# Interleaving MLP stages across batch rows and changing who transposes k and the score operand, in a fused sparse-attention and gMLP kernel

## The chip, the cores and the metric

The kernel runs on one core of one Trainium2 chip. The metric is device time in microseconds (us) of one execution. A profile is of one execution, taken by the hardware profiler; its span (first to last instruction) is 1.7 us shorter than the time of that execution. The granted TensorE clock was 0.96 to 1.00 in the mean over the span in every profile used here. The mean hides something: the clock is 1 except in stretches of 3.4 to 10.2 us in which it is 0.5, and there matmuls of 512 columns start about 427 ns apart in place of 216.

Engine names are those of the profile: PE is TensorE's matmuls and PEld its weight loads, DVE is VectorE, ACT is ScalarE, POOL is GpSimd, SP is SyncE, which only issues DMAs here.

## The reference, cut to what matters

```python
# batch 4, heads 8, sequence 768, head_dim 64; chunks of 32 keys, the 6 best chunks of 24 are kept per query
k_min, k_max = min and max of k over each chunk
ub     = sum over d of max(q * k_min, q * k_max)          # an upper bound of a chunk's score
keep   = the 6 chunks with the largest ub, among the causal ones
scores = q k^T / 8, masked to kept chunks and to causal pairs
x      = softmax(scores) v                                # (4, 768, 512) after joining the heads

h      = relu(x @ w_in)                                   # 512 -> 1024, split into u and v
v_n    = layer norm of v without scale
gated  = u * (w_spatial @ v_n + b_spatial)                # 768 x 768 along the sequence
out    = gated @ w_out                                    # 512 -> 512, float32
```

The kernel handles the 32 heads as 16 pairs. Four pairs make one batch row of attention, and each row then goes through the MLP. So the MLP of row b runs beside the attention of row b+1, and the MLP of the last row runs alone at the end.

## The kernel before: the parts that the change and the argument touch

Work is written as small functions that are hung on "beats", 12 to a pair; a scheduler orders each engine's instructions from them. The parts of one pair that matter are these (cuts are marked with `# ...`):

```python
NB = 4
kh_ring = [[ring.tile([P, S], F16, name=f"kh{i}_{hi}") for hi in range(2)] for i in range(NB)]
later = cp.tile([P, 2, 2 * NCH - CPT], F16)
# ...
def init_kh(i):                       # constant half of the key operand
    for hi, (d0, d1) in enumerate(HALF):
        nc.sync.dma_start(out=kh_ring[i][hi][d0:d1, :], in_=expand)

def k_transpose(self):                # pairs 0 to 5 on PE, the rest by DMA transpose from SP
    if self.i < 6:
        self.kT = kT = ps_ml.tile([P, S], F16, tag="mlp", name="kTp")
        for t in range(NQT):
            nc.tensor.transpose(kT[:, t * P:(t + 1) * P], self.k[:, t], identity)
    else:
        self.kT = sb.tile([P, S], F16, tag="kT", name="kT", bufs=3)
        nc.sync.dma_start_transpose(out=self.kT..., in_=self.k...)

def k_max(self):                      # k_min likewise; both on DVE
    nc.vector.tensor_reduce(self.kmm[:, 0, :], self.kT..., axis=AX.X, op=Alu.max)

def a_transpose(self, hi):            # score operand (query and chunk selection): PE, then ACT copies it to SBUF
    self.tr = self.trans_tile()
    for t in range(NQT):
        nc.tensor.transpose(self.tr[:, t * P:(t + 1) * P], self.qs[:, t, 2 * hi:2 * hi + 2, :], identity)

def triangle(self, hi):               # causal mask on the diagonal blocks; row 0 does it on PE instead
    if self.b == 0:
        return
    # ...
    nc.gpsimd.affine_select(out=blk, in_=blk, ...)

def x_transpose(self):
    # ...
    if 4 <= self.i < NPAIR - 1:
        nc.sync.dma_start_transpose(out=dst..., in_=self.x16...)     # xT, read by the MLP's v and u groups
    else:
        # six PE transposes and a DVE copy
```

All loads of q, k, v and of the weights convert float32 to float16 and are issued from POOL, which also runs the triangles. All DMA transposes (k, xT, and the gated product's gT) and the output stores are issued from SP, in one queue.

The MLP of a row is a list of steps: per 128 rows a v group (4 matmuls, ACT relu, DVE statistics), a u group (4 matmuls, ACT relu), an s group (6 matmuls, DVE gate, DMA transpose gT) and an o group (4 matmuls, ACT copy, store). They are spread evenly over the 48 beats of the next row's attention:

```python
for ti in range(NQT): v_group(ti)
for ti in range(NQT):
    u_group(ti)
    if ti >= 1: norm_group(ti - 1)
norm_group(NQT - 1)
for ti in range(NQT): s_group(ti)
for ti in range(NQT): o_group(ti)          # with a lag of 4 beats
# ...
first, count = (b + 1) * HP * BEATS + 9, HP * BEATS
```

Buffers: three PSUM buffers (`ps_ml`) that the MLP groups rotate through.

The softmax here doesn't subtract the row's maximum and nothing guards it: scores larger than these inputs give would overflow.

## Time and profile before

| | before |
|---|---|
| median time | 223.69 us at first, 224.07 us with a fourth run (223.66 to 225.91) |
| span of the profile | 221.8 us |
| PE, DVE, ACT, POOL busy | 88%, 69%, 74%, 36% |

The first lines are from the page of the kernel before: span, busy time by engine, two rows in 40 equal slices of 5.5 us (the granted clock and the busy share of the DMA engines, in tenths, where 9 is 90% or more), and the chain of waits that ended last, by engine.

```profile
span 221.8 us, 5296 instructions
PE 194.7 (88%) x2022; PEld 118.6 (53%) x2022; DVE 153.0 (69%) x453; ACT 163.8 (74%) x335; POOL 80.3 (36%) x99
...
PEclk9999999997999999999999999999999999999998
DMA  6999999999999999967992059428210334520375
...
PE 44%; DMA 18%; DVE 17%; ACT 9%; POOL 7%; issue 3%; POOLq 0%; ACTq 0%; DVEq 0%; SPq 0%
```

The DMA engines are full for about 100 us, then have room.

Busy time of PE overstates its work, because matmuls overlap: one of 512 columns is shown 379 ns long in the mean, but the next starts 216 ns after it. "PE work" below is the number of matmuls times the spacing at which they start when nothing holds them: 216 ns for 512 columns, 162 for 384, 108 for 256, 102 for 240, 56 for 128, and 25 and 29 to 30 for the 48 and 65 columns of the small ones. These are read from the instruction timeline. All 2022 matmuls of the kernel before make about 180 us.

The next view is the table of stretches of the kernel before: start and end, length, and the busy time and count of each engine. The cuts are the first exponential of pair 0, 4, 8 and 12 and the last exponential of all.

```profile
0.00:16.50 16.50, 5.64 (x52) 4.50 (x53) 8.58 (x29) 4.73 (x7) 15.28 (x24) 1.00 1.50 130
16.50:49.90 33.40, 29.54 (x443) 22.75 (x442) 27.09 (x88) 29.39 (x63) 23.75 (x33) 1.00 2.19 162
49.90:99.40 49.50, 44.26 (x489) 27.43 (x489) 45.43 (x133) 38.32 (x84) 21.10 (x22) 0.97 1.99 146
99.40:145.60 46.20, 44.47 (x470) 26.36 (x469) 34.46 (x110) 40.19 (x86) 12.38 (x12) 1.00 0.83 104
145.60:187.40 41.80, 41.69 (x419) 24.43 (x418) 23.38 (x69) 36.82 (x75) 6.95 (x8) 1.00 0.35 77
187.40:221.80 34.40, 29.11 (x156) 13.14 (x154) 14.10 (x28) 14.39 (x27) 0.86 (x1) 0.98 0.42 119
```

The five pairs of columns after the length are PE, PEld, DVE, ACT and POOL; then follow the granted clock, the DMA share and GB/s. I call these stretches the start, the no-MLP stretch, the third, fourth and fifth stretch, and the tail. In the third stretch DVE is busy 45.4 of 49.5 us.

Views of waits, here and below, are cut to the lines that the text uses; `...` marks lines left out between or before them. The last view is who waited for whom between 46 and 64 us in the kernel before, when pair 4 is at work: total us, times, longest.

```profile
POOL w_out_sb L355 <- DMA vt_80<-in_v_dram: 4.2, 1, 4.2
ACT e L263 <- PE sc L258: 3.8, 2, 2.2
PEld L281 <- POOL e L270: 2.7, 1, 2.7
PE acc L281 <- POOL e L270: 2.2, 1, 2.2
DVE kmm L177 <- DMA kT<-k: 2.2, 1, 2.2
```

There are two trails in it. DVE stood for the transposed k of pair 6, which took 9.9 us from issue to landing. POOL stood 4.2 us in the issue of a weight load, and PE later stood 2.2 us for POOL's triangle.

### The profile page before, as it was taken

The numbers are of one execution on the slowest core, as the hardware profiler recorded it, in microseconds if no ns is written. First come the engines' busy times: TensorE is split into PE (matmuls) and PEld (weight loads), VectorE is DVE, ScalarE is ACT, GpSimd is POOL, SyncE is SP. The second block draws the span as 40 slices with busy tenths as digits, with TensorE's granted clock in tenths as the row PEclk, the third lists the DMA queues.
The fourth block names the chain that finished last, engine by engine and source line by source line (L and its number), as shares of the span: only waits on it lengthen the run. The fifth ranks groups of instructions, "written<-read, shape, count | busy, mean of one in ns | idle before, by whom it ended". The sixth has DMA issues, their size and how long they took to land.

```text
span 221.8 us, 5296 instructions
## 1 busy us (share of the span) xinstructions
PE 194.7 (88%) x2022; PEld 118.6 (53%) x2022; DVE 153.0 (69%) x453; ACT 163.8 (74%) x335; POOL 80.3 (36%) x99
## 2 busy tenths in 40 slices
PE   0377999887699989999799999999999999999990
PEld 0266776664366655556455565666555655444430
DVE  6455998968689999998469967773478354376510
ACT  2416999996598888589799997799999876576033
POOL 7992688692695263107111241111111122000000
PEclk9999999997999999999999999999999999999998
DMA  6999999999999999967992059428210334520375
GB/s 39 184 166 150 134 174 150 185 178 147 167 153 161 145 137 138 162 96 126 202 213 57 3 42 114 82 52 210 109 40 1 38 71 92 206 95 0 75 130 224
DMA packets 111273, 26.89 MB, mean 121 GB/s; under 512 B 105872, under 2 KB 107664, under 8 KB 111248
## 3 DMA queue, kind: packets, MB, share of 16 engines
q0 software_dynamic: 76512, 12.19, 84.7%
q1 hardware_dynamic: 34736, 14.36, 33.4%
q8 instruction: 16, 0.26, 0.5%
q14 instruction: 9, 0.07, 0.1%
HBM read 24.38 MB, written 6.29 MB: 138 GB/s over the span
## 4 chain that ended last, share of the span: by engine, by line
PE 44%; DMA 18%; DVE 17%; ACT 9%; POOL 7%; issue 3%; POOLq 0%; ACTq 0%; DVEq 0%; SPq 0%
PE mlp L380 27%; PE sc L258 7%; DMA k<-in_k_dram 7%; PE acc L281 5%; DMA kT<-k 4%; ACT e L263 4%; DMA gT<-g 3%; DVE kmm L177 3%; DMA xT<-x_1868 3%; DVE kmm L181 2%; ACT o L429 2%; PE tr L244 2%; POOL qs_83 L330 2%; DVE vn L404 1%; POOL k L321 1%
## 5 line engine op out<-in xcount | busy, mean ns | idle before, releaser
L263 ACT ACTIVATE e<-sc 128x512 f16<-128x512 f32 x192 | 98.0, 557 | 19.2 <-PE sc L258 16.2
L380 PE MATMUL mlp<-w_in_sb,xT 128*128 128x512 f16 x192 | 51.8, 379 | 1.2 <-DMA xT<-x_1868 1.2
L270 POOL TENSOR_SCALAR_AFFINE_SELECT e<-e 128x768 f16<-128x768 f16 x24 | 21.5, 896 | 81.5 <-ACT e L263 81.4
L281 PEld LDWEIGHTS <-e 128*128 128x128 f16 x672 | 31.2, 98 | 19.5 <-POOL e L270 2.7
L380 PE MATMUL mlp<-vn,wsT 128*128 128x512 f16 x144 | 39.1, 379 | 0.0
L419 DVE SCALAR_TENSOR_TENSOR g<-mlp,b_col,u 128x512 f16<-128x512 f32 x24 | 17.9, 748 | 12.8 <-PE mlp L380 11.5
L380 PE MATMUL mlp<-w_out_sb,gT 128*128 128x512 f16 x96 | 26.0, 379 | 0.0
L380 PEld LDWEIGHTS <-xT 128*128 128x128 f16 x192 | 17.0, 98 | 15.2 <-DMA xT<-x_1868 1.7
L429 ACT COPY o<-mlp 128x512 f32<-128x512 f32 x24 | 14.1, 590 | 14.2 <-PE mlp L380 10.5
L392 DVE BATCH_NORM_STATS2 stats<-vraw 128x6 f32<-128x512 f32 x24 | 16.6, 691 | 8.2 <-ACT vraw L390 8.1
L390 ACT ACTIVATE vraw<-mlp 128x512 f32<-128x512 f32 x24 | 14.4, 600 | 5.3 <-PE mlp L380 5.3
L380 PEld LDWEIGHTS <-wsT 128*128 128x128 f16 x144 | 12.9, 97 | 10.1
L319 POOL DMA_DIRECT2D k<-in_k_dram x14 | 14.5, 1051 | 4.2 <-DMA kT<-k 1.7
L412 ACT ACTIVATE u<-mlp 128x512 f16<-128x512 f32 x24 | 14.8, 619 | 1.4 <-PE mlp L380 1.4
L281 PE MATMUL acc<-vt_80,e 128*128 128x65 f16 x252 | 14.1, 195 | 1.2 <-DVE x_1662 L289 0.8
L281 PE MATMUL acc<-vt_81,e 128*128 128x65 f16 x252 | 12.9, 194 | 1.2 <-DVE x_984 L289 1.2
L404 DVE TENSOR_SCALAR vn<-vraw,mv,rstd 128x512 f16<-128x512 f32 x24 | 13.1, 602 | 0.6 <-ACT rstd L402 0.6
L380 PEld LDWEIGHTS <-gT 128*128 128x128 f16 x96 | 8.6, 97 | 7.5 <-DMA gT<-g 0.8
L288 DVE RECIPROCAL rec<-acc 128x6 f32<-128x6 f32 x32 | 5.9, 186 | 8.8 <-PE acc L281 8.6
L261 PE MATMUL sc<-tri,identity 128*128 128x128 f16 x48 | 11.1, 232 | 0.0
L220 PEld LDWEIGHTS <-rq 128*128 128x128 f16 x160 | 8.4, 99 | 5.1 <-issue 2.1
L177 DVE TENSOR_REDUCE kmm<-kT 128x24 f16<-128x768 f16 x10 | 9.4, 941 | 2.2 <-DMA kT<-k 2.2
(225 smaller groups left out, 379.2 us busy)
## 6 DMA issues: line engine op xcount, KB each, us to landing
out_dram<-o SPq DMA_DIRECT2D x24, 256.0 KB, 2.3
k<-in_k_dram POOLq DMA_DIRECT2D x14, 192.0 KB, 11.1
vt_80<-in_v_dram POOLq DMA_DIRECT2D x3, 384.0 KB, 9.3
qs_84<-in_q_dram POOLq DMA_DIRECT2D x6, 192.0 KB, 8.9
vt_81<-in_v_dram POOLq DMA_DIRECT2D x3, 384.0 KB, 10.0
ws_raw<-in_moe_w_spatial_dram POOLq DMA_DIRECT2D x6, 192.0 KB, 7.7
w_in_sb<-in_moe_w_in_dram POOLq DMA_DIRECT2D x8, 128.0 KB, 5.4
qs_85<-in_q_dram POOLq DMA_DIRECT2D x4, 192.0 KB, 8.6
```

Of the source, the lines that this page charges most:

```text
L177: nc.vector.tensor_reduce(self.kmm[:, 0, :], self.kT.rearrange("d (c ch) -> d c ch", ch=CHUNK), axis=AX.X, op=Alu.max)
L258: mm(sc[:, col:col + n], lhsT=self.kh[hi][:, t * P:(t + 1) * P], rhs=self.a[hi][:, q0:q0 + n], start=True, stop=not diag)
L263: nc.scalar.activation(out=self.e[hi][:, g * 512:g * 512 + width], in_=sc[:, 0:width], func=Act.Exp, scale=scale)
L270: nc.gpsimd.affine_select(out=blk, in_=blk, compare_op=Alu.is_ge, fill=0.0, base=0, channel_multiplier=-1, pattern=[[0, NQT], [1, P]])
L281: mm(self.av[:, qi, :], lhsT=self.e[hi][:, c:c + P], rhs=self.v[hi][:, t, 0:D + 1], start=first and n == 0, stop=last and n == len(blocks) ...
L319: nc.gpsimd.dma_start(out=t[:, :, :, 1 - hi, :].rearrange("p x t d -> p (x t) d"), in_=source(k, b, h, 2))
L380: mm(st[group][:, 0:cols], lhsT=lhsT, rhs=rhs, start=(j == 0), stop=(j == n - 1))
L392: nc.vector.bn_stats(stats, st["vraw"][:, ti, :])
L404: nc.vector.tensor_scalar(st["vn"][:, ti, :], in0=st["vraw"][:, ti, :], scalar1=st["mv"][:, ti, 0:1], scalar2=st["rstd"][:, ti, :], op0=Al ...
L412: nc.scalar.activation(st["u"][:, ti, :], h, func=Act.Relu)
L419: nc.vector.scalar_tensor_tensor(g, in0=vs, scalar=b_col[:, ti:ti + 1], in1=st["u"][:, ti, :], op0=Alu.add, op1=Alu.mult)
L429: nc.scalar.copy(o_sb, o_ps)
```

## The change

Its intent: make the score operand by DMA in the second half, where the DMA engines have room, and take k off the DMA engines, which are full in the first half; put the output matmuls of a row between the v groups of the next row; and do three small things (one mask matmul per pair for five, a cheaper start of the key operand, later weight loads). Cut to its core:

```diff
     def init_kh(i):
+            if i < 2:
+                nc.scalar.copy(kh_ring[i][hi][d0:d1, :], expand)
+            else:
+                nc.sync.dma_start(out=kh_ring[i][hi][d0:d1, :], in_=expand)
-            nc.sync.dma_start(out=kh_ring[i][hi][d0:d1, :], in_=expand)

         def k_transpose(self):
-            if self.i < 6:
+            if self.i < 16:

         def bounds(self):
+            mm(ub[:, 0:(NQT - 1) * W], lhsT=sub_chunk, rhs=later, start=True, stop=False)
             for qi in range(1, NQT):
                 # ... two matmuls per qi
-                mm(ub[:, (qi - 1) * W:qi * W], lhsT=sub_chunk, rhs=later[:, :, ...], start=False, stop=True)

         def a_transpose(self, hi):
+            if hi == 0:
+                self.a = sb.tile([P, NQT, 2, P], F16, tag="a", name="a")
+            if self.i >= 8:
+                if hi == 0:
+                    nc.sync.dma_start_transpose(out=self.a..., in_=self.qs...)
+                return
         # ... a_copy returns at once for those pairs

-        for ti in range(NQT): v_group(ti)      # ... u, norm, s, o of one row after the other
+        return v_, u_, n_, s_, o_
+    pending = [[] for _ in range(NQT)]
     for b in range(B):
+        v_, u_, n_, s_, o_ = mlp(b)
+        steps = sum(pending[:2], [])           # two o groups of the row before
+        for ti in range(NQT):
+            steps += v_[ti]
+            if ti + 2 < NQT:
+                steps += pending[ti + 2]       # the other four between the v groups
+        # ... u with norm, then s; o only for the last row
+        pending = o_
-        first, count = (b + 1) * HP * BEATS + 9, HP * BEATS
+        first, count = (b + 1) * HP * BEATS + 13, HP * BEATS

-        at(12 + 8 * j, load_w_in, j)           # and w_spatial 36 -> 44, w_out 62 -> 76,
+        at(20 + 8 * j, load_w_in, j)           # spatial transposes 60 + 2 so -> 66 + 3 so
```

## The prediction

> **What bounds it now.** The page has TensorE (PE) busy 88%, but busy overstates it, so I price its 2022 matmuls by the start-to-start spacing in the timeline: 216 ns for 512 columns, 56 for 128, 30 for 65, 25 for 48. The Trainium skill ("TensorE: Matmul & The Clock Gate", Back-to-back issue gap) gives N/2.4 + 2.5 ns; the trace agrees at 512 and 128. Sum: 180 us of the 222 us span; granted clock 0.99. The rest is 16 us of start, about 5 us of output at the end, and stalls. By stretches between the first exponentials of pairs 0, 4, 8, 12 and the last exponential (timeline, windows):
>
> - 0–16.5: start.
> - 16.5–49.9 (no MLP): ScalarE busy 29.5, PE work 24.
> - 49.9–99.4: VectorE busy 45.9, ScalarE 38, PE work 41. VectorE bounds it; idle time includes 2.2 us for a k transpose by DMA that took 9.9 us (in the chain).
> - 99.4–145.6: PE work 42.9, ScalarE 40.3; 3.3 us lost, partly on an xT transpose by DMA of 6.1 us (in the chain).
> - 145.6–187.4: PE work 41.0.
> - 187.4–221.8: MLP alone, about 29 us PE work at 216 ns a matmul, then evictions and stores.
>
> **What the change does.**
>
> - PE: 96 query transposes go, 60 k transposes come, 80 small mask matmuls become 16 of 240 columns (102 ns each, estimate from the spacing): −5.4 + 3.4 − 0.4 = −2.4 us net.
> - ScalarE: 16 copies of about 0.8 us go; four 64x768 copies come in the start, where it waits anyway.
> - VectorE: 20 key operand copies read PSUM (about 0.54 us) instead of SBUF (often 0.36, up to 0.9): up to +3.
> - DMA: ten k transposes and four operand loads leave the saturated first half (DMA row full to about 105 us); eight double-sized query transposes come, each with about ten beats (10 us) to land. Weight loads go later, so q, k, v come sooner and the triangle on POOL waits less behind DMA issues.
> - Interleaving moves MLP work, it does not remove it. By the instruction order of both kernels, PE work in the four stretches goes 24→24, 40→36, 43→40, 41→39, and in the tail 29→36. VectorE's work in the third stretch falls from about 47 to 40 us (same durations), because fewer gates and fewer k reductions lie there. Output matmuls no longer follow right behind their gT transposes, and v groups get four more beats for xT.
>
> **Sum.** Start 16.5→16.3; no-MLP 33.4→33; VectorE-bound 49.5→43; next 46.2→42; next 41.8→39.7; tail 34.4→41. Span 215, time about **216.5 us** (−3.2%), range **211.5 to 220.5**. Faster by over 2%: 0.75; within 2%: 0.21; slower: 0.04. The tail gives back more than half of what the attention stretches gain.
>
> **Right or wrong would show as:** last exponential near 174 us (now 187.4); tail about 6.5 us longer with PE spacing still 216 ns; no wait for a k transpose by DMA, and the xT wait after 100 us gone; ScalarE busy down about 10 us; PE stalls in the third stretch still several us, since VectorE and not PE bounds it.
>
> **What could make it wrong.** Query transposes by DMA landing later than ten beats, above all pairs 8 and 9 while loads still fill the DMA engines, or queued behind other SP issues: scores would wait. Every k tile now holds one of the three PSUM buffers that MLP groups rotate through, so matmuls could wait for evictions. VectorE reading k from PSUM could lengthen the third stretch. If DMA supply binds the first 100 us, lighter DMA gains more than I count. Tail stalls at the v/o interleave would add to the end.

## More of the kernel before

Most runs of one kernel lie within about 1% of each other here, and the ratios compare runs of the state "fast" alone. Two runs of the kernel before were "slow" (227.24 and 226.51 us); they count only in the medians of the column "before, same rounds".

The chain, followed back from the last instruction, spends only 44% of the span on PE, though PE is "88% busy". It spends 18% on DMAs and 17% on DVE.

Pair 5 began 13.4 us after pair 4, with 7.4 us of PE work in between.

## The result, and the profile after

The changed kernel took 211.72 us (median of 4 runs, 210.93 to 212.05) against 224.07 us. A ratio is the mean time of one kernel's fast runs over that of the other's in the same rounds, so it is not quite the ratio of the medians: 0.943, with a 95% interval of 0.937 to 0.949. That is a gain of 5.7%, where 3.2% was forecast.

From the page of the changed kernel, the same lines as before:

```profile
span 209.2 us, 5074 instructions
PE 187.0 (89%) x1922; PEld 114.8 (55%) x1922; DVE 154.1 (74%) x453; ACT 155.7 (74%) x323; POOL 79.6 (38%) x99
...
PEclk9999999999999999999999999999999999999998
DMA  6999999999999699979998932948792115530365
...
PE 65%; ACT 17%; DVE 5%; POOL 5%; DMA 4%; issue 3%; POOLq 0%; ACTq 0%
```

DVE does as much as before and PE only slightly less (about 177 us of work against 180). What changed is the chain: DMA went from 18% to 4% of the span, DVE from 17% to 5%, and PE from 44% to 65%. The stretches of the changed kernel, cut at the same events and with the same columns:

```profile
0.00:16.70 16.70, 5.66 (x49) 4.50 (x50) 8.60 (x29) 8.04 (x12) 15.49 (x24) 1.00 1.48 111
16.70:49.20 32.50, 27.93 (x430) 21.41 (x428) 28.81 (x98) 29.51 (x63) 23.34 (x32) 1.00 2.27 164
49.20:89.00 39.80, 38.35 (x468) 25.60 (x468) 36.18 (x115) 35.44 (x77) 21.48 (x24) 1.00 1.94 138
89.00:130.00 41.00, 40.53 (x429) 24.37 (x426) 36.46 (x109) 34.72 (x76) 11.77 (x13) 1.00 1.10 142
130.00:169.20 39.20, 38.97 (x378) 22.45 (x375) 26.11 (x74) 33.40 (x72) 6.63 (x8) 1.00 0.60 112
169.20:209.20 40.00, 35.60 (x188) 16.48 (x186) 17.89 (x33) 14.57 (x26) 0.86 (x1) 0.98 0.42 119
```

Against the prediction's sum:

| stretch | before | predicted | after | after minus predicted |
|---|---|---|---|---|
| start | 16.5 | 16.3 | 16.7 | +0.4 |
| no MLP | 33.4 | 33 | 32.5 | −0.5 |
| third | 49.5 | 43 | 39.8 | −3.2 |
| fourth | 46.2 | 42 | 41.0 | −1.0 |
| fifth | 41.8 | 39.7 | 39.2 | −0.5 |
| tail | 34.4 | 41 | 40.0 | −1.0 |
| span | 221.8 | 215 | 209.2 | −5.8 |

More than half of the miss lies in the third stretch. Of its four pairs, pair 4 alone went from 13.4 us to 6.8. The waits between 46 and 64 us in the changed kernel show why:

```profile
POOL w_out_sb L366 <- DMA vt_80<-in_v_dram: 1.8, 1, 1.8
...
PE sc L269 <- ACT e L274: 0.9, 3, 0.4
...
ACT e L274 <- PE sc L269: 0.7, 3, 0.3
```

Neither a wait of DVE for k nor one of PE for a triangle is left.

### The profile page after: what moved, and what is told of

It reads as the page before. It is cut to its first block, busy times and chain, and to the rows that moved or that the text cites. A ratio compares the mean times of both kernels' runs of the same rounds, so it can differ in the third digit from the quotient of the medians.

```text
span 209.2 us, 5074 instructions
## 1 busy us (share of the span) xinstructions
PE 187.0 (89%) x1922; PEld 114.8 (55%) x1922; DVE 154.1 (74%) x453; ACT 155.7 (74%) x323; POOL 79.6 (38%) x99
## 4 chain that ended last, share of the span: by engine, by line
PE 65%; ACT 17%; DVE 5%; POOL 5%; DMA 4%; issue 3%; POOLq 0%; ACTq 0%
PE mlp L391 38%; PE sc L269 11%; ACT e L274 9%; PE acc L292 8%; ACT a L260 3%; DMA k<-in_k_dram 3%; PE ub L225 2%; POOL qs_83 L341 2%; PE kTp L173 2%; PE tr L208 1%; DVE vn L415 1%; POOL k L332 1%; ACT o L440 1%; DMA out_dram<-o 1%; ACT u L423 1%
## 5 line engine op out<-in xcount | busy, mean ns | idle before, releaser
L391 PE MATMUL mlp<-w_in_sb,xT 128*128 128x512 f16 x192 | 52.9, 379 | 0.0
L281 POOL TENSOR_SCALAR_AFFINE_SELECT e<-e 128x768 f16<-128x768 f16 x24 | 20.8, 867 | 68.7 <-ACT e L274 68.6
L391 PE MATMUL mlp<-vn,wsT 128*128 128x512 f16 x144 | 37.3, 379 | 0.0
L391 PE MATMUL mlp<-w_out_sb,gT 128*128 128x512 f16 x96 | 25.1, 379 | 0.0
L391 PEld LDWEIGHTS <-wsT 128*128 128x128 f16 x144 | 12.9, 98 | 10.4
L181 DVE TENSOR_REDUCE kmm<-kTp 128x24 f16<-128x768 f16 x16 | 15.1, 945 | 3.4 <-PE kTp L173 3.2
L423 ACT ACTIVATE u<-mlp 128x512 f16<-128x512 f32 x24 | 14.3, 597 | 1.7 <-PE mlp L391 1.5
L185 DVE TENSOR_REDUCE kmm<-kTp 128x24 f16<-128x768 f16 x16 | 15.1, 943 | 0.0
L173 PE MATMUL kTp<-identity,k 128*128 128x128 f16 x96 | 8.6, 230 | 6.3 <-POOL tri L144 5.9
L391 PEld LDWEIGHTS <-gT 128*128 128x128 f16 x96 | 9.1, 98 | 8.9
L415 DVE TENSOR_SCALAR vn<-vraw,mv,rstd 128x512 f16<-128x512 f32 x24 | 11.8, 544 | 2.2 <-ACT rstd L413 2.1
```

What stands on the lines that cost most here:

```text
L181: nc.vector.tensor_reduce(self.kmm[:, 0, :], self.kT.rearrange("d (c ch) -> d c ch", ch=CHUNK), axis=AX.X, op=Alu.max)
L185: nc.vector.tensor_reduce(self.kmm[:, 1, :], self.kT.rearrange("d (c ch) -> d c ch", ch=CHUNK), axis=AX.X, op=Alu.min, negate=True)
L281: nc.gpsimd.affine_select(out=blk, in_=blk, compare_op=Alu.is_ge, fill=0.0, base=0, channel_multiplier=-1, pattern=[[0, NQT], [1, P]])
L391: mm(st[group][:, 0:cols], lhsT=lhsT, rhs=rhs, start=(j == 0), stop=(j == n - 1))
L423: nc.scalar.activation(st["u"][:, ti, :], h, func=Act.Relu)
```

## The experiments

Two lists of kernels were made: the kernel before with one part of the change alone (b_), and the changed kernel with one part undone (u_) or with something new (n_). The table holds the result of every run. "Pair 4" is the time from the first exponential of pair 4 to that of pair 5, with the PE work in it in brackets; "pair 8" likewise. The tail is what follows the last exponential. Kernels of one block ran together on one chip, with the kernel before in the same rounds; compare across blocks by the ratio.

| run | median us | before, same rounds | ratio (95%) | pair 4 | pair 8 | third stretch | tail |
|---|---|---|---|---|---|---|---|
| before | 224.07 | | 1 | 13.4 (7.4) | 13.3 (11.4) | 49.5 | 34.4 |
| changed | 211.72 | 224.07 | 0.943 (0.937–0.949) | 6.8 (4.9) | 9.6 (9.7) | 39.8 | 40.0 |
| b_k | 223.17 | 224.84 | 0.995 (0.988–1.003) | 9.4 (7.6) | 16.0 (11.3) | 45.5 | 33.6 |
| b_a | 223.81 | 224.84 | 0.998 (0.992–1.004) | 14.3 (6.7) | 20.2 (10.7) | 50.6 | 33.5 |
| b_mlp | 221.49 | 224.84 | 0.988 (0.983–0.994) | 10.9 (5.0) | 9.8 (9.4) | 45.7 | 41.3 |
| b_w | 225.09 | 224.84 | 1.003 (0.995–1.011) | 16.2 (6.7) | 12.7 (11.4) | 52.2 | 34.3 |
| u_mlp | 216.23 | 224.03 | 0.965 (0.958–0.972) | 9.3 (7.7) | 16.2 (10.8) | 45.4 | 33.4 |
| u_a | 219.18 | 224.03 | 0.978 (0.973–0.984) | 6.8 (4.9) | 10.5 (10.4) | 40.7 | 41.0 |
| u_k | 222.05 | 224.03 | 0.990 (0.982–0.997) | 14.5 (4.9) | 8.7 (8.5) | 49.2 | 40.4 |
| u_small | 213.33 | 224.03 | 0.952 (0.945–0.959) | 7.7 (5.8) | 9.6 (9.7) | 40.0 | 40.3 |
| u_mlp_x | 214.05 | 224.89 | 0.952 (0.949–0.956) | 9.3 (7.7) | 13.0 (11.2) | 45.5 | 33.4 |
| u_k_tri | 226.55 | 224.89 | 1.008 (1.005–1.012) | 9.9 (6.5) | 8.8 (8.5) | 51.3 | 41.0 |
| n_k12 | 218.85 | 224.89 | 0.972 (0.968–0.976) | 6.8 (4.9) | 10.0 (9.7) | 46.0 | 41.5 |
| n_a4 | 223.24 | 224.89 | 0.994 (0.989–0.998) | 7.6 (4.9) | 9.9 (9.8) | 45.3 | 40.7 |
| n_k12b | 212.77 | 225.98 | 0.942 (0.936–0.947) | 6.8 (4.9) | 10.0 (9.7) | 39.9 | 41.3 |
| n_kb | 211.73 | 225.98 | 0.938 (0.932–0.944) | 6.8 (4.9) | 9.6 (9.7) | 39.9 | 40.1 |
| u_mlp_o | 216.54 | 225.98 | 0.957 (0.949–0.965) | 9.3 (7.7) | 16.5 (10.8) | 45.7 | 32.5 |
| u_mlp_xo | 211.64 | 225.98 | 0.937 (0.932–0.942) | 9.3 (7.7) | 11.7 (11.2) | 46.0 | 32.6 |
| n_ob | 210.09 | 224.63 | 0.936 (0.932–0.940) | 6.8 (4.9) | 9.6 (9.7) | 39.9 | 39.2 |
| n_after | 211.40 | 224.63 | 0.942 (0.938–0.945) | 6.8 (4.9) | 9.6 (9.7) | 39.9 | 40.0 |

Some matmul records can be missing from a trace, so the work in brackets can be a few tenths off.

### One part alone, on the kernel before

**b_k** — every k transpose on PE:

```diff
-            if self.i < 6:
+            if self.i < 16:
```

> The kernel before with only one thing of the change: every k transpose on PE. Theory A (the sum of the prediction: a stretch lasts as long as the work of its busiest engine): PE gains 60 transposes at 56 ns (+3.4 us) and VectorE reads k from PSUM, nothing else is removed, so 223 to 227 us, and pair 5 still begins about 13 us after pair 4. Theory B (the lost time around 50 to 63 us is a head-of-line wait: VectorE, which works in order, stood 2.2 us before a k reduction for a DMA transpose that took 9.9 us, and everything behind it came late): 217 to 222 us, with pair 5 beginning 8 to 11 us after pair 4 in place of 13.4.

**b_a** — the score operand by DMA transpose from the ninth pair on, with the methods `a_transpose` and `a_copy` and the operand of `scores` as in the change:

```diff
+            if self.i >= 8:
+                if hi == 0:
+                    nc.sync.dma_start_transpose(out=self.a..., in_=self.qs...)
+                return
```

> The kernel before with only the score operand by DMA transpose from the ninth pair on (and its one-tile layout). Takes 96 PE transposes (5.4 us) and 14 to 16 ScalarE copies of 0.8 us away, both in the stretches after about 99 us. Theory A and B alike: 218 to 221 us if PE work is what those stretches follow; the stretches before 99 us unchanged within 1 us. If DMA transposes land too late for the scores, 223 us or more.

**b_mlp** — the function `mlp` and the loop that places its steps as in the change (o groups between the next row's v groups, `+ 13` for `+ 9`), weight loads as before.

> The kernel before with only the MLP order of the change (output matmuls between the v groups of the next row, start four beats later). Theory A: it moves about 30 matmuls from the attention stretches to the tail; the third stretch, bound by VectorE, gains from 4 fewer gates there (3 us), the fourth loses its wait for xT (2 us), the tail grows by 6.5 us: 220 to 224 us. Theory B: the wait around 50 to 63 us stays as it was, since k still comes by DMA, so pair 5 still begins 12 to 14 us after pair 4; total 219 to 224 us.

**b_w** — only the weight loads later:

```diff
-        at(12 + 8 * j, load_w_in, j)              # w_spatial 36 -> 44, w_out 62 -> 76
+        at(20 + 8 * j, load_w_in, j)
-        at(5 * BEATS + 2 * so, prep_w_spatial, so)
+        at(66 + 2 * so, prep_w_spatial, so)
```

> The kernel before with only the later weight loads (and the spatial weights' transposes 6 beats later). Theory A: no engine's work changes, so 223 to 225 us. Theory B in its second form (the first triangle on POOL stood behind weight-load issues that waited for DMA, and PE waited 2.2 us for it at 60 us): the first triangle starts 2 to 5 us earlier than 59.7 us and the total is 220 to 222.5 us.

Measured: 0.995, 0.998, 0.988 and 1.003. Of the four, only b_mlp is clearly faster, and by 1.2%. Together they explain about 1.6 of the 5.7%. So neither theory of that round held as a whole.

- b_k did cure pair 4 (9.4 us with 7.6 of work), and its third stretch fell by 4 us. Then pair 8 took 16.0 us where it had taken 13.3, and the fifth stretch grew by 1.1 us, with 3.9 us more of DVE busy and 0.3 of PE work. The total fell in theory A's range, the pair in theory B's.
- b_mlp was expected by theory B to leave pair 4 at 12 to 14 us, since k still came by DMA. It took 10.9, with 5.0 us of PE work in place of 7.4. Its total fits both theories, so it did not tell them apart.
- b_a took 96 matmuls from PE and 16 copies of about 0.8 us from ACT and gained nothing. Its total fits the branch "land too late for the scores", but the waits below are others. Pair 8 took 20.2 us with 10.7 us of PE work.
- b_w speaks against the prediction's guess on the weight loads, as far as the kernel before goes. The first triangle came at 61.3 us, later than the 59.7 of the kernel before.

What b_a ran into is in its waits between 94 and 122 us, and in the row of the clock on its page:

```profile
...
POOL qs L336 <- DMA a<-qs: 8.1, 1, 8.1
PEld L388 <- DMA xT<-x: 7.0, 1, 7.0
PE mlp L388 <- DMA xT<-x: 6.5, 1, 6.5
ACT o L437 <- DMA out_dram<-o: 6.1, 1, 6.1
```

```profile
PEclk9999999999769999999967999999999999999999
```

At the change from one row to the next, the first v group needs the last xT of the row at once. That transpose stands in SP's queue behind a k transpose, the new and twice as large score operand, and the first two of the row's six output stores: its input was complete at 103.9 us, it was issued at 109.7 and landed at 114.8. PE stood 6.5 us for it. ACT stood 6.1 us because its output copy had no free buffer until a store landed. Then the clock was at half from 113.6 to 120.4 us. Much of the saving was handed back here; pair 4 took 0.9 us longer than before as well, with the clock at half from 59.0 to 65.8 us.

The Trainium skill ("DMA: Bandwidth & Descriptors", DMA Transpose (X-bar)) says that a plain DMA transpose can be issued from SyncE or ScalarE only, and its section on silent corruption says that two streams that transpose at once can corrupt each other. That is a reason to have all of them in one queue; no run here tests it.

### One part undone, on the changed kernel

**u_mlp** — the MLP order and the `+ 9` put back, with `at(66 + 2 * so, prep_w_spatial, so)` so that the spatial weights are ready before their reader.

> The changed kernel with only the MLP order and start put back (spatial weights' transposes two beats apart so that they stay ahead of their reader). The parts alone gave -0.5, -0.2, -1.2 and +0.3 per cent, together far less than the 5.7 of the whole. Theory A (parts add up, the rest sits in the small parts): this loses about 1.2 per cent, 213 to 216 us. Theory C (without the interleave the first v group of a row stands right behind the last xT transpose of that row, which waits in the one in-order DMA queue behind the other transposes and stores; what k and a gain is given back there as a PE wait): 217 to 223 us, with pair 9 beginning 13 us or more after pair 8 (9.6 in the changed kernel) and a PE wait for xT of 2 us or more in that stretch.

**u_a** — the score operand of every pair by PE and ACT:

```diff
-            if self.i >= 8:          # in a_transpose and in a_copy
+            if self.i >= 16:
```

> The changed kernel with the score operand of every pair by PE and ScalarE again. Theory A (alone it was worth 0.2 per cent): 211 to 213 us. Theory C (it is worth its PE work of 5.4 us once nothing else is waited for): 215 to 219 us, all of the loss between the first exponential of pair 8 and the last exponential, the third stretch (pairs 4 to 7) within 1.5 us of the changed kernel's 39.9.

**u_k** — k by DMA again from the seventh pair on:

```diff
-            if self.i < 16:
+            if self.i < 6:
```

> The changed kernel with k transposed by DMA again from the seventh pair on. PE has 60 transposes (3.4 us) less. Theory A (alone k on PE was worth 0.5 per cent): 212 to 214 us. Theory C: both k and the doubled query transposes now stand in one queue while loads still fill the DMA engines; pair 5 again begins 10 us or more after pair 4 (6.7 in the changed kernel), total 215 to 222 us; but after about 130 us, when the DMA engines have room, its stretch is shorter than the changed kernel's 39.2 by up to 1 us.

**u_small** — the mask matmuls of `bounds` (with `later`) and `init_kh` put back as before.

> The changed kernel with the mask matmuls of the bounds and the start of the key tiles put back (80 small matmuls, eight DMAs from SBUF at the start). Both theories: PE +0.4 us and at most 1 us at the start, 211 to 213.5 us. If the small parts carry what the four big parts do not explain (about 4 per cent), 217 us or more.

Undoing a part costs far more than doing it alone gains. From 211.72 us, undoing k costs 10.3 us, the score operand 7.5, the MLP order 4.5 and the two small parts 1.6 (all by medians; the changed kernel itself ran in an earlier block, with the kernel before at 224.07 there and 224.03 here). These add to 24 us, twice the gain of the whole. So the parts are not terms of a sum. Each clears a wait that would otherwise swallow what the others free.

Against the expectations: u_a (219.18 us) is just above its range, and most of its loss lies between the start of pair 8 and the last exponential, as expected (6.3 of 8.5 us of span; third stretch 40.7 us against 39.8). u_k (222.05) is at the upper edge of its range. u_small (213.33) is within its range, though its first two stretches lost 1.6 us and not at most 1.

u_k is the clearest case. The first line is its third stretch, with the columns of the tables of stretches; the rest are its waits between 46 and 66 us.

```profile
48.60:97.90 49.30, 40.06 (x447) 25.83 (x447) 39.99 (x127) 36.17 (x80) 23.36 (x26) 0.93 2.19 150
```

```profile
...
POOL w_out_sb L366 <- DMA vt<-in_v_dram: 5.1, 1, 5.1
PEld L292 <- POOL e L281: 3.6, 1, 3.6
PE acc L292 <- POOL e L281: 3.4, 1, 3.4
DVE kmm L181 <- DMA kT<-k: 3.4, 1, 3.4
```

The stretch lasts 49.3 us while no engine is busy for more than 40.1. In the changed kernel the same stretch lasts 39.8 us, with 4 us less on DVE. So the stretch was not long because DVE had much to do. The two trails of the kernel before are back, and pair 4 takes 14.5 us with 4.9 us of PE work. The clock of 0.93 in the first line is two stretches of half clock in pair 4 (54.0 to 57.5 and 60.9 to 64.3 us).

u_mlp missed my range by being better than 217 us. Its pair 8 took 16.2 us as expected, but I had named the wrong wait: between 92 and 112 us, its trace puts the loss to the output copies.

```profile
...
ACT o L440 <- DMA out_dram<-o: 3.7, 1, 3.7
...
PE mlp L391 <- ACT o L440: 3.2, 1, 3.2
```

### Which wait, and is it a queue or the DMA engines?

**u_mlp_x** — u_mlp, with xT of pair 7 (the last pair of the second row) by PE:

```diff
-            if 4 <= self.i < NPAIR - 1:
+            if 4 <= self.i < NPAIR - 1 and self.i != 7:
```

> The changed kernel with the MLP order put back, as in the earlier run (216.2 us, pair 9 began 16.2 us after pair 8), and one transpose more moved: xT of pair 7, the last pair of the first MLP row's successor, goes by PE (six transposes, 0.34 us) in place of DMA. Theory C (the row hand-over waits for the last xT in the DMA queue): pair 9 begins 10 to 12.5 us after pair 8, no PE wait for that xT, total 211 to 213.5 us. If the hand-over is slow for another reason (order of the MLP work itself): no change, 215 to 217 us.

**u_k_tri** — u_k, with the triangles of pairs 4 and 5 by PE as in the first row:

```diff
-                diag = self.b == 0 and si == 0
+                diag = self.i < 6 and si == 0
         def triangle(self, hi):
-            if self.b == 0:
+            if self.i < 6:
```

> The changed kernel with k by DMA again from the seventh pair on (222.0 us, pair 5 began 14.5 us after pair 4), and for pairs 4 and 5 the triangle masked on PE as in the first row (24 small matmuls, 1.3 us) in place of POOL. Splits the two waits of pair 4: the trace of the run without this has VectorE waiting 3.4 us for kT (then PE 2.4 us for VectorE) and later PE waiting 3.4 us for POOL's triangle, which stood behind a weight load's issue. If the triangle is its own loss: pair 5 begins 10 to 12 us after pair 4, total 218 to 220.5. If both hang on the late k: still 13 us or more, total 221 to 224.

**n_k12** — k by DMA from the thirteenth pair on:

```diff
-            if self.i < 16:
+            if self.i < 12:
```

> The changed kernel with k by DMA from the thirteenth pair on (transposes after about 105 us, when the loads are nearly done): PE has 24 transposes (1.3 us) less, VectorE reads k from SBUF. If k by DMA only hurts while the loads fill the DMA engines: 209.5 to 211.5 us against 211.7. If it hurts anywhere (queue shared with score operand, xT, gT and stores): 213 us or more.

**n_a4** — the score operand by DMA from the fifth pair on:

```diff
-            if self.i >= 8:          # in a_transpose and in a_copy
+            if self.i >= 4:
```

> The changed kernel with the score operand by DMA from the fifth pair on, in place of the ninth: 48 more PE transposes (2.7 us) and 8 more ScalarE copies (6.4 us) go, but these four transposes of twice k's size would be issued from about 40 to 75 us, when the DMA row is full. By the prediction's fear: scores wait, 213 to 219 us. If landing stays under ten beats: 208 to 210 us.

u_mlp_x came out at 214.05 us, 0.6 us outside my range, with pair 8 at 13.0 us. Moving one transpose of 0.34 us of PE work was worth 2.2 us by medians. The waits left there are still output copies that wait for stores.

u_k_tri is a plain miss: 226.55 us, slower than both alternatives. Pair 4 fell to 9.9 us, so the triangle's wait was real. But pair 5 then took 20.2 us: DVE stood 6.4 us for a k by DMA, and PE 6.8 us for DVE's selection. Removing one wait only let the next one come out. The waits of pair 5 begin with a k that lands late.

n_k12 was meant to be harmless and was not: 218.85 us. That fits the branch "if it hurts anywhere" in number, but most of its loss (4.6 of 8.4 us of span) lies at pair 6 (15.8 us against 11.2), before the first k that it transposes by DMA is read (101.2 us). These are its waits between 66 and 86 us:

```profile
POOL k L330 <- DMA kT<-k: 7.5, 1, 7.5
POOL e L281 <- ACT e L274: 6.2, 2, 4.6
ACT e L274 <- PE sc L269: 5.0, 1, 5.0
PEld L292 <- POOL e L281: 4.2, 1, 4.2
PE acc L292 <- POOL e L281: 4.0, 1, 4.0
```

The scheduler had put the k transposes of pairs 12 and 13 early, at 71.1 us, where the DMA engines are full. POOL, about to issue the k load of the last two pairs, stood 7.5 us until 76.0 us, when those transposes gave their k buffer back. It then issued four loads and reached the triangle of pair 6 only at 80.7 us, though that had had its input since about 74 us. PE stood 4.0 us for it. That reading can be tested, because a fourth buffer takes the wait away without touching the order of the DMAs (next section).

n_a4 took 223.24 us, some 4 us beyond the worse of its two ranges. It shows that the prediction's first fear is real, at another place than feared: two score operands landed too late and PE stood 10.9 us for them, as its waits between 44 and 80 us show.

```profile
...
PE sc L269 <- DMA a<-qs: 10.9, 2, 6.0
```

In the changed kernel, with the operands from the ninth pair on, PE never waited for one (the largest such wait, of PEld, was 0.2 us). They landed 3.7 to 8.4 us after issue; in n_a4 the slowest took 11.4.

### Taking the waits away by buffers

These runs were made because the cause of the prediction's miss was still open: full DMA engines as such, or in-order queues that pass one late landing on.

**n_k12b** — n_k12 with a fourth k buffer. **n_kb**, the control — the changed kernel with a fourth k buffer.

```diff
-... tag="k", name="k", bufs=3)
+... tag="k", name="k", bufs=4)
```

> k by DMA from the thirteenth pair on, as in the run that took 218.9 us, and a fourth buffer for k. There POOL stood 7.5 us before a k load for a DMA transpose to give a k buffer back, with a triangle behind it in its queue, and PE waited 4.0 us for that triangle (pair 7 began 15.8 us after pair 6, 11.2 in the changed kernel). Theory D (in-order queues turn one late landing into waits of other engines): with the buffer free POOL does not stand still, pair 7 begins 10.5 to 12.5 us after pair 6, total 209.5 to 213 us. If the DMA engines' load by itself is what costs: still 216 us or more.

> The control for the run above: the changed kernel with a fourth k buffer and nothing else. Loads of k can go out earlier and compete with other loads: 210.5 to 212.5 us, within 1 us of the changed kernel's 211.7.

**u_mlp_o** — u_mlp with six output buffers. **u_mlp_xo** — u_mlp_x with six output buffers.

```diff
-                o_sb = ml.tile([P, DM], F32, tag="o", name="o", bufs=3)
+                o_sb = ml.tile([P, DM], F32, tag="o", name="o", bufs=6)
```

> The changed kernel with the MLP order put back (216.2 us, pair 9 began 16.2 us after pair 8), and six output buffers in place of three. There ScalarE stood 3.7 us before an output copy for a store to land and PE 3.2 us for that copy to free a PSUM buffer. If these stores are the hand-over's loss: pair 9 begins 11 to 13 us after pair 8, total 212 to 214 us. If the xT transpose behind them is (its removal alone gave 214.1): 214.5 to 216.5 us.

> Both at once: MLP order put back, xT of pair 7 by PE, six output buffers. If queue waits are all that the interleave saves: pair 9 begins 10.5 to 12 us after pair 8 and the total is 210.5 to 213 us, within 1 us of the changed kernel. If the order of the MLP work has a worth of its own (less VectorE and PE work beside the third stretch): 213 us or more, with the third stretch still about 45 us against 39.9 and the tail 33 against 40.

The buffer alone does nothing (n_kb: 211.73 us), but under n_k12 it takes 6 us off (218.85 to 212.77; ratios 0.972 and 0.942). Pair 6 is back at 11.2 us, and POOL's waits between 66 and 86 us in n_k12b name no k transpose any more:

```profile
POOL e L281 <- ACT e L274: 9.8, 3, 4.3
POOL qs L339 <- PE tr L254: 2.3, 1, 2.3
...
ACT e L274 <- PE sc L269: 0.7, 2, 0.4
```

The DMA transposes stayed, and the loss went. So at this spot the DMA engines' load was only the cause of a late landing; the time was lost in POOL's queue. That the engines carry out their queues in order is stated by the Trainium skill ("TensorE: Matmul & The Clock Gate", the note on queue depths under "Architectural detail": ScalarE, VectorE and GPSIMD are strict FIFO). These traces agree: the triangle, whose input had been there since about 74 us, started at 80.7 us, after the load that waited until 76.0 us and all that stood behind that in POOL's queue. With the fourth buffer the same load went out at 63.4 us, without such a wait.

The hand-over of rows needed both cures. Six output buffers alone gave nothing (216.54 us), because the wait turned up at the next thing in line: PE then stood 3.7 us for xT, as the waits of u_mlp_o between 92 and 112 us show.

```profile
...
PE mlp L391 <- DMA xT<-x: 3.7, 1, 3.7
```

With both, pair 8 took 11.7 us for 11.2 us of work, and the kernel with the old MLP order took 211.64 us, as fast as the changed kernel with a fourth k buffer in the same rounds (211.73). About 0.8 us of that is the shorter tail that six output buffers give by themselves (32.6 against 33.4). The fairer match is the changed kernel with six output buffers (n_ob below, in other rounds): the ratios to the kernel before are 0.937 and 0.936. So the interleave is worth its 4.5 us almost entirely by what it puts between the last xT and its reader, and by spacing out the stores. The work that it moves from the third stretch (45.4 to 39.8 us) it pays back in the tail (33.4 to 40.0), as predicted.

### A version that beats both

**n_ob** — the changed kernel with six output buffers. **n_after** — the changed kernel again, as its control in the same five rounds.

> A version meant to beat both kernels: the changed kernel with six output buffers in place of three, and nothing else. In the two runs of the old MLP order with six buffers the part after the last exponential was 32.5 and 32.6 us, with three buffers 33.4 in both: the last output copies no longer wait for the stores before them. Expected: tail 39.2 us against 40.1, total 0.6 to 1.2 us below the changed kernel in the same rounds, and the attention stretches unchanged.

> The changed kernel itself, as the control of the same rounds: 210.9 to 212.1 us as measured before.

n_ob took 210.09 us against 211.40 us; their ratios to the kernel before, 0.936 and 0.942, differ by 0.6%. No run of one lies among those of the other (209.69 to 210.50 against 210.91 to 211.87), and the gain of 1.3 us is just over the 0.6 to 1.2 expected. In the control ACT's last output copies wait for a store before they can begin:

```profile
203.21 0.59 ACT L440 COPY o<-mlp 128x512 f32<-128x512 f32 x1 [0.28 <-PE mlp L391]
205.27 1.79 ACT L440 COPY o<-mlp 128x512 f32<-128x512 f32 x3 [1.48 <-DMA out_dram<-o]
```

In n_ob the copies begin 0.86 us apart, with 0.28 us of idle time before each, so that the last copy no longer comes in a row of three:

```profile
204.37 0.59 ACT L440 COPY o<-mlp 128x512 f32<-128x512 f32 x1 [0.28 <-DMA out_dram<-o]
205.23 0.59 ACT L440 COPY o<-mlp 128x512 f32<-128x512 f32 x1 [0.28 <-PE mlp L391]
```

The columns of these timelines are start, duration, engine, instruction, count, and in brackets the idle time before it and what ended it.

## Why the prediction was right or wrong, point by point

**Right: the direction and the cost of the parts on PE.** PE work fell by 2.4 us, as counted: the trace has 36 matmuls of 128 columns and 80 of 48 less, and 16 of 240 more, at the spacings given above. The spacing stayed at 216 ns for 512 columns, as the formula of the Trainium skill has it (N/2.4 + 2.5 ns, "Back-to-back issue gap").

**Right: the interleave moves work and does not remove it.** The tail grew from 34.4 to 40.0 us (41 was predicted). The waits for a k transpose by DMA and for xT are gone from the changed kernel. ACT's busy time fell by 8.1 us; "about 10" was said.

**Wrong, and the step that failed: "VectorE bounds it", in the sum "VectorE-bound 49.5→43".** It became 39.8, which is 3.2 of the 5.8 us of span that the sum was off. The term had two pieces: 40 us of VectorE work and 3 us lost. Measured were 36.2 us of work and 3.6 us lost. So as a term of the sum its work was mis-sized. I priced it from the instruction order with typical durations, "from about 47 to 40"; the traces show 45.4 and 36.2 us (43.9 and 37.7 if the stretch is cut at the reciprocals in place of the exponentials). That the same pricing was too high for the kernel before could have been seen at once.

**Why it failed: VectorE's work does not set the length of this stretch.** u_k has 40.0 us of DVE work in it, just what I priced, and takes 49.3 us; b_k has 39.4 and takes 45.5. What made the stretch long in the kernel before was k that arrived late, engines that work in order behind it, and the slow clock that came with the waits. The prediction saw the first of these waits (2.2 us at DVE) and booked it at 2.2 us. Pair 4 alone lost 6 us to it and to what followed, and putting k back on DMA in the changed kernel costs 10.3 us. The chain of waits had said so: 18% of the span on DMAs. What the length goes with, where no such wait is left, is PE's own work: in all twelve kernels with k of every pair or of the first twelve pairs on PE, except n_k12 and n_a4 with the waits shown, the stretch is about 4 to 5 us longer than its PE work (about 36 to 42 us). The prediction had that work right (36 us) and did not use it. No run varies PE's work in this stretch and leaves DVE's alone, so that PE bounds it now is likely and not shown.

**The clock.** This was overlooked in the prediction and in the expectations. Every stretch of half clock before the last exponential begins while PE stands idle for 1.2 us or more, or at most 1.6 us after that; not every such idle time is followed by one (the 2.2 us at 58.4 us in the kernel before are not). An estimate of what such stretches add is the PE work started in them, at full-speed spacing: 1.7 us in the kernel before, about 6 in b_a, 5.1 in u_k (3.3 of it in the third stretch), 2.3 in n_k12, 1.7 in u_mlp, and nothing in the changed kernel, n_k12b and u_mlp_xo. With it the sums nearly close: the 20.2 us of pair 8 in b_a are 10.7 of work, 6.5 of waiting and 2.9 of slow clock; the 6.1 us that the fourth buffer takes off n_k12 are 4.0 of waiting and 2.3 of slow clock. So a wait of PE cost more here than its own length. No run separates the two.

**Wrong: adding the parts up.** I costed each part as a term. Alone, the four parts that I tried give between −1.2% and +0.3%; of the changed kernel, the three large ones undone one at a time cost between 4.5 and 10.3 us, and the two small parts together 1.6 (the weight loads were not put back). A sum cannot give both.

**Wrong: "Weight loads go later, so q, k, v come sooner and the triangle on POOL waits less behind DMA issues."** b_w gave 1.003 and a later first triangle. The triangle comes early when k is on PE: at 56.4 us in b_k, 52.8 in the changed kernel, 60.5 in u_k. A likely link is that loads land sooner without the k transposes among them; the issue-to-landing view has these medians for the kernel before, and then for b_k:

```profile
k<-in_k_dram POOLq DMA_DIRECT2D x14, 192.0 KB, 11.1
```

```profile
k<-in_k_dram POOLq DMA_DIRECT2D x14, 192.0 KB, 8.1
```

The Trainium skill ("DMA: Bandwidth & Descriptors", Arbitration) says that each DMA engine goes round its queues packet by packet, so that transposes and loads share it. The medians agree with that, but no run took the transposes' packets away and kept everything else.

**The fears.** A late score operand did not happen in the changed kernel and did happen in n_a4. Matmuls that wait for PSUM buffers because k now holds one: PE's waits in the changed kernel name no MLP matmul that waits for an eviction. Slower reading of k from PSUM: DVE's busy time rose by 1.1 us over the whole span, where up to 3 was said. The last exponential came at 169.2 us, where "near 174" was said. PE stood 3.9 us in the third stretch (39.8 us for 35.9 of work), where "still several us" was said. The tail's stalls did not come; its error of 1.0 us is the end after the last matmul, 4.4 us against 5.3 in the kernel before.

**Smaller terms.** The fourth and fifth stretch came out 1.0 and 0.5 us shorter than priced, because almost no PE stall was left (41.0 us for 40.1 of work, 39.2 for 38.6). The cheaper start of the key operand and the single mask matmul were worth more than the 0.6 us of both early terms together: without them the first two stretches take 1.6 us longer (the no-MLP stretch 33.9 us in u_small against 32.5).

**What stays open.** Weight loads were not put back in the changed kernel, so whether their shift matters there is not known. How much of k's 10.3 us is due to landing late and how much to slowing the loads was not separated: u_k_tri shows only that its waits follow each other. And n_k12b, with 24 transposes less on PE, was 1 us slower than its control; its fourth stretch took 41.9 us with 40.4 us of DVE busy (36.4 in the control), which was not followed further.

## What to carry to other kernels

When the chain of waits spends much of the span on DMAs while an engine looks busy, do not cost a change by engine work alone: look for the in-order queue in which a late landing holds up work that others need, and count the wait at all of them, and with it the time at a lower clock after PE has stood. Parts that each remove one of several waits in a row must be judged together and by undoing them one at a time, since alone they may show almost nothing, as here. Where such a wait is for a buffer, one more buffer is the cheapest test of the reading, and here twice also a cure.

## What the Trainium skill lacked or had wrong

- "TensorE: Matmul & The Clock Gate", Back-to-back issue gap: it gives a sustained spacing of about 131 ns for 512 columns and 81 ns for 128 in a real stream of weight loads and matmuls, and calls N/2.4 + 2.5 the isolated figure. Here the long stream of the tail (109 matmuls of 512 columns in 23.54 us, each with its weight load) ran at 216 ns, and rows of 128-column transposes at 55 to 56 ns; the formula fits, the two sustained figures do not.
- "Advanced Engine Details and Errata", X-Bar Transpose (TRN2): it calls transposing DMAs as fast as regular ones. No run here compares the two under the same load, so this is neither confirmed nor refuted: in the kernel before, a store of 256 KB landed in 2.3 us in the median, a k transpose of 128x768 float16 (196,608 bytes) in 2.8 us at best and 7.8 in the median. What the page lacks is how long a transpose takes to land while loads fill the DMA engines, and that is what this kernel turned on: 7.6 to 10.9 us for the first five.
- No page says what an in-order queue costs when one engine both issues loads and computes: POOL stood 7.5 us for a buffer, PE 4.0 us for the masking behind it (n_k12), and a fourth buffer returned 6 us.
